# First key unit of an attention–MLP kernel loaded in two transfers, and fewer idle matmuls on TensorE at the start

## The chip, the cores and the metric

The kernel runs on one NeuronCore of a Trainium2 chip. The metric is device time in microseconds (us), from the start to the end of one launch. Five engines run side by side, each through its own list of instructions in order, and meet only through semaphores: TensorE (PE; its weight loads, PEld, overlap its matmuls), VectorE (DVE), ScalarE (ACT), GpSimd (POOL) and SyncE (SP), which issues nearly all transfers. The transfers run on 16 DMA engines.

## The reference

Attention with random features, then an MLP with softplus, all in float32:

```python
proj = np.einsum('bhsd,md->bhsm', x, omega)      # x = q*scale or k*scale
h = proj - np.sum(x * x, axis=-1, keepdims=True) / 2.0
h = h - np.max(h, axis=-1, keepdims=True)
phi = np.exp(h) / np.sqrt(m)
...
kv = np.einsum('bhsm,bhsd->bhmd', k_p, v)        # k_p = phi(k), q_p = phi(q)
z = np.sum(k_p, axis=2)
num = np.einsum('bhsm,bhmd->bhsd', q_p, kv)
den = np.einsum('bhsm,bhm->bhs', q_p, z)[..., None] + 1e-06
x = num / den                                    # attention, heads side by side
h = x @ w_in
out = (softplus(h)) @ w_out
```

There are 8 batches of 8 heads, 576 positions of 64 columns, 128 features; the MLP has 4608 tokens, 512 columns in and out and 2048 hidden columns. For one head of keys or queries a row needs its projection (a matmul), its norm (squares, then a sum) and the largest projection of the row before the exponential can run.

## The kernel before

Four heads form a *quad*; a batch has two quads (0 and 1 of batch 0 come first). The 576 positions of a quad are cut into five *units* of 128 positions (the last has 64). A unit of keys of batch 0 goes through this chain:

- SP loads it into one tile `xk` of 128 x 772 floats (`load`, L463): columns 0 to 255 are the keys transposed, for the projection; columns 256 to 511 are the keys in rows, for the norm; the rest are the values. One transfer, 386 KB.
- PE projects it (`project`, L491): four matmuls into two banks of PSUM, `ppk ... _0` and `_1`. The two banks come from a common store of eight.
- ACT (or POOL) squares the rows (L474, L476), DVE sums them (L481).
- DVE takes the maxima of the two banks (L541, twice), then two small steps (L548, L553) give the bias of the exponential.
- ACT runs the exponentials, two for each bank (L561). They write over the unit's tile, and a bank is free for a later unit when its two are done.
- PE multiplies the exponentials with the values (`outer`, L700 and L695, into `kt`, which takes one more bank).

Units come in the order quad 0 unit 0, quad 1 unit 0, quad 0 unit 1, quad 1 unit 1 and so on. In the names of the rows below, `xk_1_0` is quad 1, unit 0. After the ten units of keys come ten of queries (`xq`, `ppq`), mixed with the weights of the MLP (`rawi`, `rawo`, split into high and low parts on ACT at L373, L381 and L391 and on DVE at L375, L385, L391 and L394). Later batches and the MLP (L1049 to L1051 and L1109 to L1111) take the rest of the time; the loads of all of it follow on SP's one queue. The kernel keeps eight semaphores for transfers in turn, so SP issues a transfer only when the one eight places before it has landed.

The order on each engine is not written by hand: `in_order` plays the works against a table of costs and due times and gives one list, and each engine's part of it is fixed when the program is built. After that, `with_fill` puts idle matmuls (`fill`, L1582) ahead of a work of PE where the planner's own clock sees a gap: `n = int((t - last - FILL) / 0.2135)`, and for works before `DENSE` (12 us by that clock) which take a bank two more. They write into a bank that is free, or into the one that the work takes, and nobody reads them. Ten more stand in front of the first projection (`fill("at.0", 10, idle)`); those multiply a tile of zeros, the others the identity. `in_order` knows nothing of the fills.

Of the kernel before, what the change touches and what calls it, by code (L numbers as in the profile page):

```python
# [35 lines left out]
MARGIN = 0.0000  # L36
START = {"SP": 0.75, "ACT": 1.9, "PE": 4.6}
SLOW = 7.19
FILL = 0.3
DENSE = 12  # L40
PATIENCE = {"PE": 0.0000, "DVE": 0.00, "ACT": 0.1822, "POOL": 0.00, "SP": 3.0950}
LEAN = {"DVE": 0.2675, "POOL": 0.1608, "ACT": 0.00}
SPREAD = ((0, 10.51), (17, 12.01))
VW = 512 + 4 * (D + 1)
# [17 lines left out]
def by(key, due):  # L62

    return due + DUE[key][PHASE[0]]
# [192 lines left out]
def with_fill(out, held, banks, until, emit):  # L257

    last, all_ = None, []
    for i, w in enumerate(out):  # L260
        if w.engine == "PE":
            t = w.end - w.cost
            n = int((t - last - FILL) / 0.2135) if last is not None and t < until else 0
            if last is not None and t < DENSE and w.take:
                n += 2
            names = [
                b for b in banks if all(x1 <= last and g < i or x0 >= t and f >= i for x0, x1, f, g in held.get(b, []))
            ] if n > 0 else []
            names = names or [box[key] for _, box, key in w.take if box[key] in banks]
            if names and n > 0:  # L270
                all_.append((emit, names[0], n))
            last = w.end
        all_.append(w)
    return all_
# [3 lines left out]
def favor_softplus_kernel(ctx, tc, q0, k0, qx, kx, tx, vv, om, wi, wo, out):  # L278
    nc = tc.nc
# [10 lines left out]
    at = ctx.enter_context(tc.tile_pool(name="at", bufs=1))  # L290
# [4 lines left out]
    def bank(name, tag):  # L295
        return ps.tile([P, 512], F32, name=name, tag=tag, bufs=1)

    idle = at.tile([P, P], F32, name="idle", tag="x.0", bufs=1)
# [38 lines left out]
    def act(n, space=None):  # L337
        return (0.066 if space == PSUM else 0.105) + 0.000833 * n

    def dve(n, rate=1):  # L340
        return 0.068 + 0.001042 * n / rate
# [4 lines left out]
    def do(engine, cost, due, emit, **kw):  # L346

        on = dict(zip(engine, cost)) if isinstance(engine, tuple) else {engine: cost}
        w = Work(on, due, emit, **kw)
        works.append(w)  # L350
        return w
# [86 lines left out]
    def plan_unit(q, kind, us, due, early, other=None):  # L438

        u = us[0]  # L440
# [3 lines left out]
        if early:  # L444
            src = (k0 if kind == "k" else q0)[q.qd]
        else:
            src = (kx if kind == "k" else qx)[q.b - 1, q.qd]
        nt = 2 * len(us) if u < 4 else 2 if other else 1
        b2 = {}
        w, n = nt * P, 2 * nt  # L450
        b = {}

        def load():
            if early:

                x = const.tile([P, 2 * DM], F32, name=f"x{nm}", tag=b["x"], bufs=1)
                b["v"] = x[:, UW : UW + 4 * (D + 1)].rearrange("p (c d) -> p c d", d=D + 1)
                b["qt"] = x[:, UW : UW + 4 * P].rearrange("p (c t) -> p c t", t=P)
                b["xs"] = x[:, : 4 * D]
                b["ph"] = x[:, : n * M].rearrange("p (c m) -> p c m", m=M)  # L460
                b["raw"], b["nat"] = x[:, :w], x[:, w : 2 * w].rearrange("p (c d) -> p c d", d=D)
                if kind == "k":
                    nc.sync.dma_start(x[:, :VW], src[:, u * VW : (u + 1) * VW])  # L463
                else:
                    nc.sync.dma_start(x[:, : 2 * w], src[:, u * UW : u * UW + 2 * w])
                return
            x = at.tile([P, 2 * UW], F32, name=f"x{nm}", tag=b["x"], bufs=1)
            nc.sync.dma_start(x[:, : 2 * w], tx[other.n - NQ] if other else src[:, u * UW : u * UW + 2 * w])
            b["raw"], b["nat"] = x[:, :w], x[:, w : 2 * w].rearrange("p (c d) -> p c d", d=D)
# [52 lines left out]
        def first(e, t):  # L522
            if not t:
                for i, x in enumerate(to):
                    x["ph"] = at.tile([P, k, M], F32, name=f"ph{nm}_{i}", tag=x["phs"], bufs=1)
            (nc.scalar.copy if e == "ACT" else nc.vector.tensor_copy)(features(t), b["pr", t][:, :, 0])
# [28 lines left out]
        def exponent(j):  # L555
# [7 lines left out]
        size = P * 4 * (VW if early and kind == "k" else 2 * w)  # L563
        ld = do(
            "SP", dma(size), by("unit.load", due), load, behind=prev.get("load"),
            take=[("w" if early else "x", b, "x")], delay=DL, spare=2 if early else 0,
        )
# [27 lines left out]
        else:  # L595
# [12 lines left out]
            for t in range(nt):  # L608
# [4 lines left out]
                c = do(  # L613
                    ("ACT", "DVE"), (act(2 * M, PSUM), dve(2 * M)), by("unit.first", due), lambda e, t=t: first(e, t), after=[p], behind=e,
                    take=[] if t else phs,
                )
# [962 lines left out]
    def fill(tag, n, idle=ident):  # L1579
        t = bank("fill", tag)[:, :P]  # L1580
        for _ in range(n):
            nc.tensor.matmul(t, idle, idle, start=True, stop=True)  # L1582

    with tc.manual_schedule():
        fill("at.0", 10, idle)
        for w in with_fill(*in_order(works, room, AHEAD, MARGIN), room["any"], 70, fill):
            if isinstance(w, tuple):
                w[0](*w[1:])
                continue
            w.emit(w.engine) if len(w.on) > 1 else w.emit()  # L1590
# [99 lines left out]
```

## Time and profile before

| what | value |
|---|---|
| median of 3 runs (lowest, highest) | 1006.22 us (1006.0, 1007.1) |
| time of the profiled execution | 1006.46 us |
| its span, first to last instruction | 1004.7 us |
| busy: PE, DVE, ACT, POOL | 992.0, 805.4, 673.7, 79.8 us |
| moved | 113.81 MB, mean 113 GB/s over the span |

The span is what the rows below are taken from; 1.8 us of the execution's time lie outside it. Matmuls are pipelined and a row of PE counts idle matmuls as busy, so PE's 99% says little about how much of its time is needed. A matmul of float32 stands as two instructions in the trace (ten fills are x20). "Idle before" counts from the modelled end of the instruction ahead; on ACT and DVE instructions that follow each other overlap by some 0.1 us, start to start being shorter than their length.

### The profile page before, as it was taken

The page shows a single profiled execution, that of the slowest core. Times are in us where ns is not written, and L with a number is a line of the kernel's source. Part 1 is how long each engine was busy: PE and PEld are TensorE (multiplying, and loading weights), DVE is VectorE, ACT ScalarE, POOL GpSimd, SP SyncE. Part 2 cuts the span into 40 slices and gives each one's busy share as a digit, 9 for nine tenths or more (in the row PEclk, how much of TensorE's full clock was granted, in tenths as well). Part 3 has the DMA queues.
Part 4 walks back from the last instruction along what each step waited for, and adds up shares of the span by engine and source line. Part 5 has one row for each costly group of instructions (what it writes and reads, how often), then busy time and mean ns, then how long its engine had stood idle before and what let it go on. Part 6 is the DMA issues. An engine that isn't in the chain of part 4 may idle for free.

```text
span 1004.7 us, 17142 instructions
## 1 busy us (share of the span) xinstructions
PE 992.0 (99%) x5753; PEld 807.7 (80%) x5753; DVE 805.4 (80%) x2194; ACT 673.7 (67%) x1629; POOL 79.8 (8%) x90
## 2 busy tenths in 40 slices
PE   9999999999999999999999999999999999999998
PEld 8888888787778787887878787878788778788886
DVE  6999997988868787888888897979889846998600
ACT  6999987757677675666675756756576555777600
POOL 0113211000001000100000000100010000001000
PEclk9999999999999999999999999999999999999999
DMA  9963444443252424442343335243534121000011
GB/s 346 373 242 118 146 151 122 134 117 94 96 149 95 134 93 132 137 114 82 115 120 126 91 95 152 95 132 94 133 117 112 64 79 42 1 1 1 1 53 32
DMA packets 64334, 113.81 MB, mean 113 GB/s; under 512 B 18268, under 2 KB 37112, under 8 KB 64248
## 3 DMA queue, kind: packets, MB, share of 16 engines
q1 hardware_dynamic: 64088, 112.60, 36.1%
q8 instruction: 46, 0.75, 0.3%
q14 instruction: 40, 0.33, 0.1%
q10 hardware_dynamic: 160, 0.13, 0.1%
HBM read 85.68 MB, written 27.03 MB: 112 GB/s over the span
## 4 chain that ended last, share of the span: by engine, by line
PE 87%; DVE 6%; ACT 4%; DMA 1%; issue 1%; POOL 0%; DVEq 0%; ACTq 0%; SPq 0%
PE acc L1109 13%; PE acc L1110 12%; PE acc L1111 12%; PE h L1049 10%; PE h L1050 9%; PE h L1051 9%; PE ppk L491 3%; PE kt L655 3%; PE xp L977 3%; PE pb L1384 2%; PE ppq L516 2%; PE pc L1384 2%; PE pa L1384 1%; DMA xq<-qx 1%; PE fill L1582 1%
## 5 line engine op out<-in xcount | busy, mean ns | idle before, releaser
L1109 PE MATMUL acc<-wo,gh 128*128 128x512 f32 x512 | 204.1, 399 | 0.0
L1110 PE MATMUL acc<-wo,gh 128*128 128x512 f32 x512 | 200.2, 391 | 0.0
L1111 PE MATMUL acc<-wo,gl 128*128 128x512 f32 x512 | 199.7, 390 | 0.0
L1049 PE MATMUL h<-xh,wi 128*128 128x512 f32 (+1 forms) x512 | 190.8, 373 | 1.9 <-DVE u L1064 1.1
L1050 PE MATMUL h<-xl,wi 128*128 128x512 f32 (+1 forms) x512 | 186.1, 364 | 0.0
L1051 PE MATMUL h<-xh,wi 128*128 128x512 f32 (+1 forms) x512 | 185.8, 363 | 0.0
L1055 ACT ACTIVATE u<-h 128x512 f32<-128x512 f32 (+1 forms) x128 | 70.1, 547 | 81.4 <-PE h L1051 79.2
L1109 PEld LDWEIGHTS acc<-wo,gh 128*128 128x128 f32 x512 | 96.2, 188 | 24.9 <-issue 6.8
L1049 PEld LDWEIGHTS h<-xh,wi 128*128 128x128 f32 x512 | 96.4, 188 | 23.4 <-DVE u L1064 3.9
L1111 PEld LDWEIGHTS acc<-wo,gl 128*128 128x128 f32 x512 | 96.1, 188 | 21.2 <-DVE gl L1204 0.4
L1110 PEld LDWEIGHTS acc<-wo,gh 128*128 128x128 f32 x512 | 96.5, 188 | 15.9
L1051 PEld LDWEIGHTS h<-xh,wi 128*128 128x128 f32 x512 | 96.4, 188 | 15.4
L1050 PEld LDWEIGHTS h<-xl,wi 128*128 128x128 f32 x512 | 96.6, 189 | 13.5
L1064 DVE SCALAR_TENSOR_TENSOR u<-h,u 128x512 f32<-128x512 f32 (+1 forms) x128 | 79.2, 619 | 32.7 <-ACT u L1061 31.5
L1068 ACT CAST gh<-u 128x512 fp32r<-128x512 f32 (+1 forms) x101 | 57.2, 566 | 46.0 <-PE acc L1110 29.1
L1072 DVE TENSOR_TENSOR gl<-u,gh 128x512 fp32r<-128x512 f32 (+1 forms) x106 | 68.7, 648 | 14.9 <-ACT gh L1068 13.1
L1061 ACT ACTIVATE u<-u 128x512 f32<-128x512 f32 (+1 forms) x128 | 74.2, 580 | 3.9
L1058 ACT ACTIVATE u<-u 128x512 f32<-128x512 f32 (+1 forms) x128 | 74.3, 581 | 3.2
L887 DVE CUSTOM_DVE_ANT_0 junk<-phq,zb 128x128 bf16<-128x128 f32 (+1 forms) x228 | 67.4, 296 | 7.0 <-ACT phq L561 0.4
L538 ACT ACTIVATE phq<-phq,smq 128x128 f32<-128x128 f32 x194 | 59.5, 389 | 10.1 <-DVE smq L553 10.1
L561 ACT ACTIVATE phk<-ppk,smk 128x128 f32<-128x128 f32 x230 | 63.6, 375 | 3.3 <-DVE smk L553 3.1
L541 DVE TENSOR_REDUCE smk<-ppk 128x4 f32<-128x512 f32 (+2 forms) x80 | 46.0, 595 | 24.5 <-PE ppk L491 24.5
(217 smaller groups left out, 1764.2 us busy)
## 6 DMA issues: line engine op xcount, KB each, us to landing
xk<-kx SPq DMA_DIRECT2D x28, 512.0 KB, 3.8
xq<-qx SPq DMA_DIRECT2D x28, 512.0 KB, 3.6
fdq<-flq SPq DMA_DIRECT2D x28, 512.0 KB, 2.8
qq<-fdq SPq DMA_DIRECT2D x112, 128.0 KB, 2.9
rawi<-wi SPq DMA_DIRECT2D x16, 512.0 KB, 6.7
rawo<-wo SPq DMA_DIRECT2D x16, 512.0 KB, 10.1
out<-o SPq DMA_DIRECT2D x32, 256.0 KB, 2.1
v<-vv SPq DMA_DIRECT2D x14, 576.0 KB, 3.7
```

What stands on the lines that cost most here:

```text
L887: nc.vector.tensor_tensor_reduce(jk[r, c % jk.shape[1]], ph[r, c], q.zb[r, h], 1.0, 1e-6, ALU.mult, ALU.add, dn[r, 0, c : c + 1])
L1049: nc.tensor.matmul(b["h"], wh, xh[:, cc, t], start=cc == 0, stop=False)
L1050: nc.tensor.matmul(b["h"], wh, xl[:, cc, t], start=False, stop=False)
L1051: nc.tensor.matmul(b["h"], wl, xh[:, cc, t], start=False, stop=cc == NCC - 1)
L1055: nc.scalar.activation(b["u"], b["h"], AF.Abs)
L1058: nc.scalar.activation(b["u"], b["u"], AF.Exp, scale=-1.0)
L1061: nc.scalar.activation(b["u"], b["u"], AF.Ln, bias=1.0)
L1064: nc.vector.scalar_tensor_tensor(b["u"], b["h"], 0.0, b["u"], ALU.max, ALU.add)
L1072: (nc.vector if e == "DVE" else nc.gpsimd).tensor_tensor(b["gl"], b["u"], b["gh"].bitcast(F32), ALU.subtract)
L1109: nc.tensor.matmul(dst, gh, w2[fc][:, 0, c], start=start, stop=False, **kw)
L1110: nc.tensor.matmul(dst, gh, w2[fc][:, 1, c], start=False, stop=False, **kw)
L1111: nc.tensor.matmul(dst, gl, w2[fc][:, 0, c], start=False, stop=stop, **kw)
```

## The change

Three things change. The tile of quad 0 unit 0's keys is loaded by two transfers, columns 0 to 255 and then 256 to 771, in place of one. Six idle matmuls stand in front instead of ten. `FILL` goes from 0.3 to 1.0 and the `DENSE` rule is gone, so that the planner puts fewer idle matmuls ahead of later works.

```diff
-FILL = 0.3
-DENSE = 12
+FILL = 1.0
...
             n = int((t - last - FILL) / 0.2135) if last is not None and t < until else 0
-            if last is not None and t < DENSE and w.take:
-                n += 2
...
                 if kind == "k":
-                    nc.sync.dma_start(x[:, :VW], src[:, u * VW : (u + 1) * VW])
+                    for c in ((0, w), (w, VW)) if not q.qd and not u else ((0, VW),):
+                        nc.sync.dma_start(x[:, c[0] : c[1]], src[:, u * VW + c[0] : u * VW + c[1]])
...
-        fill("at.0", 10, idle)
+        fill("at.0", 6, idle)
```

The order of all other instructions is the same on PE, DVE, ACT, POOL and SP. Lines behind the edits move up by two or three (L491 is L489, L1582 is L1580). Three places show what moves.

PE at the start of the program, before:

```order
L1582 MATMUL fill<-idle 128x128 x10
L491 MATMUL ppk_0_0_0_115<-omf,xk_0_0_106 128x128
L491 MATMUL ppk_0_0_1_116<-omf,xk_0_0_106 128x128
L491 MATMUL ppk_0_0_0_115<-omf,xk_0_0_106 128x128
L491 MATMUL ppk_0_0_1_116<-omf,xk_0_0_106 128x128
L1582 MATMUL fill<-ident 128x128
L491 MATMUL ppk_1_0_0_130<-omf,xk_1_0_108 128x128
```

The same place after:

```order
L1580 MATMUL fill<-idle 128x128 x6
L489 MATMUL ppk_0_0_0_112<-omf,xk_0_0_102 128x128
L489 MATMUL ppk_0_0_1_113<-omf,xk_0_0_102 128x128
L489 MATMUL ppk_0_0_0_112<-omf,xk_0_0_102 128x128
L489 MATMUL ppk_0_0_1_113<-omf,xk_0_0_102 128x128
L489 MATMUL ppk_1_0_0_125<-omf,xk_1_0_105 128x128
```

Four idle matmuls are gone in front, and one between the first two projections; the two like it ahead of `xk_0_1` and `xk_1_1` are gone too. The first projection now waits for the first of the two transfers alone, by the program's semaphores.

PE from the end of the fourth projection (quad 1 unit 1) to the first product `kt`, before:

```order
L1582 MATMUL fill<-ident 128x128 x6
L491 MATMUL ppk_0_2_0_189<-omf,xk_0_2_123 128x128
L491 MATMUL ppk_0_2_1_190<-omf,xk_0_2_123 128x128
L491 MATMUL ppk_0_2_0_189<-omf,xk_0_2_123 128x128
L491 MATMUL ppk_0_2_1_190<-omf,xk_0_2_123 128x128
L1582 MATMUL fill<-ident 128x128 x5
L491 MATMUL ppk_1_2_0_216<-omf,xk_1_2_137 128x128
L491 MATMUL ppk_1_2_1_217<-omf,xk_1_2_137 128x128
L491 MATMUL ppk_1_2_0_216<-omf,xk_1_2_137 128x128
L491 MATMUL ppk_1_2_1_217<-omf,xk_1_2_137 128x128
L1582 MATMUL fill<-ident 128x128 x2
L700 MATMUL kt_0_237<-xk_0_0_106 128x65 x4
```

and after:

```order
L1580 MATMUL fill<-ident 128x128
L489 MATMUL ppk_0_2_0_175<-omf,xk_0_2_120 128x128
L489 MATMUL ppk_0_2_1_176<-omf,xk_0_2_120 128x128
L489 MATMUL ppk_0_2_0_175<-omf,xk_0_2_120 128x128
L489 MATMUL ppk_0_2_1_176<-omf,xk_0_2_120 128x128
L489 MATMUL ppk_1_2_0_196<-omf,xk_1_2_132 128x128
L489 MATMUL ppk_1_2_1_197<-omf,xk_1_2_132 128x128
L489 MATMUL ppk_1_2_0_196<-omf,xk_1_2_132 128x128
L489 MATMUL ppk_1_2_1_197<-omf,xk_1_2_132 128x128
L698 MATMUL kt_0_214<-xk_0_0_102 128x65 x4
```

Of thirteen idle matmuls one is left. Two further groups shrink later: eighteen become fifteen ahead of an MLP product near 61 us of the trace, and a single one near 72 us goes.

SP, its first transfers, before:

```order
L314 DMA omf_83<-om 128x128
L463 DMA xk_0_0_106<-k 128x772
L463 DMA xk_1_0_108<-k 128x772
L463 DMA xk_0_1_110<-k 128x772
L463 DMA xk_1_1_112<-k 128x772
```

and after:

```order
L311 DMA omf_83<-om 128x128
L461 DMA xk_0_0_102<-k 128x256
L461 DMA xk_0_0_102<-k 128x516
L461 DMA xk_1_0_105<-k 128x772
L461 DMA xk_0_1_107<-k 128x772
```

Every later transfer stands one place further back. ACT's square of the first unit waits for the second of the two.

## Rows read from the trace of the kernel before

**Rows 1.** Busy time by stage: stretch, its length, then busy (instructions) by engine, clock, DMA.

```profile
0.00:10.45 10.45, 9.17 (x58) 7.74 (x58) 4.96 (x22) 4.48 (x11) 0.70 (x6) 1.00 0.80 271
10.45:27.80 17.35, 17.18 (x154) 15.04 (x153) 14.30 (x56) 14.64 (x51) 0.80 (x2) 1.00 1.04 401
27.80:102.30 74.50, 71.54 (x597) 61.69 (x595) 72.85 (x213) 73.29 (x198) 16.70 (x15) 1.00 0.65 239
102.30:1004.70 902.40, 894.14 (x4949) 723.20 (x4948) 713.33 (x1906) 581.26 (x1371) 61.58 (x68) 1.00 0.32 96
```

**Rows 2.** Chain of waits over the first 30 us: start, length, what.

```profile
1.05 4.65 PE fill L1582 x20
...
5.75 1.20 PE ppk L491 x8
6.95 0.43 PE fill L1582 x2
...
7.42 0.72 PE ppk L491 x8
...
10.52 1.55 PE fill L1582 x12
...
12.90 1.32 PE fill L1582 x10
...
15.05 0.66 PE fill L1582 x4
...
15.75 1.11 PE kt L700 x8
...
27.82 0.39 ACT kvs L706
```

**Rows 3.** Waits of DVE and of ACT, 8 to 30 us: total, times, longest.

```profile
DVE smk L541 <- PE ppk L491: 3.2, 5, 1.1
...
ACT xk L561 <- DVE smk L553: 2.1, 3, 1.5
```

**Rows 4.** The fills' matmuls by operand: ns min/median/max, first and last start.

```profile
L1582 PE MATMUL fill<-ident x70: 271/275/377, 6.9 to 71.8; 128*128 128x128 f32 x70
...
L1582 PE MATMUL fill<-idle x20: 421/421/583, 1.1 to 5.3; 128*128 128x128 f32 x20
```

**Rows 5.** Timeline of ACT: start, length, what, idle before and what ended it.

```profile
4.54 0.42 ACT L474 ACTIVATE xk<-xk 128x256 f32<-128x256 f32 x1 [2.53 <-DMA xk<-k]
5.55 0.42 ACT L474 ACTIVATE xk<-xk 128x256 f32<-128x256 f32 x1 [0.59 <-DMA xk<-k]
...
8.47 0.42 ACT L474 ACTIVATE xk<-xk 128x256 f32<-128x256 f32 x1 [0.91 <-DMA xk<-k]
...
9.75 1.23 ACT L561 ACTIVATE xk<-ppk,smk 128x128 f32<-128x128 f32 x4
...
11.54 0.62 ACT L561 ACTIVATE xk<-ppk,smk 128x128 f32<-128x128 f32 x2 [0.26 <-DVE smk L553]
...
14.18 0.62 ACT L561 ACTIVATE xk<-ppk,smk 128x128 f32<-128x128 f32 x2 [0.37 <-DVE smk L553]
...
18.84 1.66 ACT L561 ACTIVATE xk<-ppk,smk 128x128 f32<-128x128 f32 x6 [1.48 <-DVE smk L553]
```

**Rows 6.** Timeline of DVE, the first two waits for a projection.

```profile
6.98 0.76 DVE L541 TENSOR_REDUCE smk<-ppk 128x2 f32<-128x256 f32 x2 [0.56 <-PE ppk L491]
...
12.86 0.42 DVE L541 TENSOR_REDUCE smk<-ppk 128x2 f32<-128x256 f32 x1 [1.08 <-PE ppk L491]
```

**Rows 7.** Timeline of SP's issues and of ACT, 22 to 28 us.

```profile
23.46 0.33 SPq L468 DMA_DIRECT2D xk<-kx  x1
...
25.46 0.41 ACT L474 ACTIVATE xq<-xq 128x256 f32<-128x256 f32 x1
26.38 1.14 ACT L561 ACTIVATE xq<-ppq,smq 128x128 f32<-128x128 f32 x4 [0.51 <-DVE smq L553]
```

**Rows 8.** Timeline of SP's first issues, and of DVE's first use of a transfer.

```profile
1.19 5.65 SPq L463 DMA_DIRECT2D xk<-k  x10
...
2.66 0.23 DVE L315 TENSOR_SCALAR omf<-omf 128x128 f32<-128x128 f32 x1 [1.42 <-DMA omf<-om]
```

## The prediction

> **What bounds the kernel now.** I read the busy time by stage first. The span has four stages [rows 1]. Up to 10.45 us the loads set the pace. From there to 27.8 us the chain of waits runs along PE without a break, but much of that chain is idle matmuls: ten in front (4.65 us), three single ones (0.43 us each), then groups of 1.55, 1.32 and 0.66 us between needed projections [rows 2]. From 27.8 to 102.3 us DVE is busy 72.85 and ACT 73.29 of 74.5 us: these two are the bound, and almost nothing there waits. From 102.3 us to the end PE is busy 894 of 902 us.
>
> So the question is what the change takes off before 27.8 us, and whether the two later stages pass it on. In the early stretch the waits say who holds whom: between 8 and 30 us DVE waits for nothing but projections, 3.2 us in five waits, and ACT waits 2.1 us for the biases that DVE makes of them [rows 3]. PE is what is late, and PE is late because it runs idle matmuls: that is the reader's first result. A fill marks PE busy in the trace while the data for the next projection has long landed.
>
> **The change part by part. In front.** Ten idle matmuls take 4.65 us, 0.465 each; four fewer end 1.86 us sooner, near 3.8 us. The first projection then needs the first 128 KB of its unit. From below: 64 KB issued at 0.74 us are used at 2.66 us, 1.9 us later [rows 8]; the new first transfer, issued near 1.2 us, can't land much before 3.1 us. From above: the whole unit is there at 4.54 us [rows 5]. I take 3.4 us, nearer to the small transfer. The projection runs from 3.9 to 5.1 us (1.20 us as before [rows 2]) in place of 5.75 to 6.95 us.
>
> What is that worth? Little. DVE takes the maxima of the first projection only behind the sum of the second unit's squares, and that unit lands at 5.55 us; square and sum end near 6.4 us. DVE's wait of 0.56 us before 6.98 us [rows 6] goes, no more. Without the split the projection would run from 4.6 to 5.8 us, still before 6.4 us. And ACT's square at 8.47 us has waited 0.91 us for its transfer [rows 5]: up to there landings are the bound, and nothing done on PE moves them. I cost the split and the four fills at nothing; the landings hide them, and 0.56 us is the most that they are worth.
>
> The split's price: one more issue on SP. Ten issues of keys take 5.65 us [rows 8], so each later key is issued 0.5 us later, onto a queue that is ahead of its transfers: units land 1.0 us apart or more from 4.54 us on [rows 5], and the sixth is issued before the second has landed. Between 0 and 0.5 us on every later landing; I take 0.1 us, because the queue is full, and allow nothing below zero, since the bytes are the same.
>
> **From 8.47 us to 18.84 us.** Here ACT is the engine to follow. It has three waits, 0.26, 0.37 and 1.48 us, 2.11 us in all [rows 5]. Six exponentials take 1.66 us at 18.84 us, so they start 0.25 us apart and are 0.39 us long; a wait counted from the end of the one ahead hides that overlap of 0.14 us, three times. Without waits ACT stands at 18.84 - 2.11 - 0.42 = 16.3 us, 2.5 us sooner. Do the three biases come in time?
>
> - The first (11.54 us) needs DVE 0.4 us sooner. DVE has won the 0.56 us above. Yes.
> - The second (14.18 us) hangs on the fifth projection. It stood behind six fills, from 10.52 to 12.07 us [rows 2]. Its two banks are free when the first two of the four exponentials at 9.75 us are done, near 10.4 us [rows 5]. So its last three matmuls now run from 10.4 to about 11.05 us, and DVE's maxima start at 11.2 us in place of 12.86 us [rows 6]; the bias is 1.6 us sooner and ACT wants it 0.9 us sooner. Yes.
> - The third (18.84 us, after 1.48 us) hangs on the seventh. Ahead of it now: sixth projection, whose second bank ACT gives back at 12.16 - 0.37 = 11.8 us, done at 12.45 us; the first product `kt`, whose bank comes 0.8 us later, 12.65 to 13.75 us (15.75 to 16.86 us before [rows 2]); then the seventh, done at 14.6 us in place of 17.5 us. DVE's steps between it and the bias took 1.25 us, so 15.85 us; ACT is free at 16.3 us. In time, with 0.45 us to spare.
>
> So ACT gains 2.5 us, PE 2.9 us, and PE no longer holds anyone. DVE could gain 2.9 us, but its work on the first weights (L385) follows ACT's (L381): 2.5 us for it too.
>
> **What is late next: landings.** The loads keep the DMA queues full (share 1.04 [rows 1]) and don't move. SP's issue at 23.46 us waited for the transfer eight places ahead, the queries that ACT squares at 25.46 us [rows 7]: 2.0 us of slack, so ACT's gain falls to 2.0 us there. But ACT then waited 0.51 us for a bias at 26.38 us. Its start is now 23.45 + 0.3 by the landing, 26.38 - 2.5 = 23.9 by the bias: the 2.5 us are back.
>
> **The sum.** 2.5 us, less 0.1 us for later landings: 2.4 us. Upper end: ACT's waits up to 26.38 us altogether, 2.5 + 0.5 = 3.0 us. Lower end, with 0.5 us for the landings: 2.0 us. From 27.8 to 102.3 us DVE and ACT are full and in fixed order, so they pass a shift on, and transfers that wait for buffers follow; the fewer fills near 61 and 72 us cost and give nothing, since the bound there is DVE (at most four of them, 1 us, if it were PE). From 102.3 us PE passes it on. The profiled execution takes 1006.46 us; 2.4 us less is 1004.06 us. The median lies 0.24 us below the profiled one, 1006.22 us: I forecast **1003.8 us**.
>
> **The rivals. TensorE's clock stays low for longer.** The row says: the fills in front last 421 ns, later ones 275 ns [rows 4]; the first projection 1.20 us, the second 0.72 us [rows 2]. [...] Now PE pauses at 5.1, 6.8 and 7.9 us and later. Up to 10.4 us a low clock is free: projections of 1.2 us fit between landings. [...]
>
> [...]
>
> [...]
>
> **The split delays all keys.** If two transfers cost the queue the full 0.5 us, ACT's row at 8.47 us moves by that and 2.0 us are left: 1004.2 us. Against it: landings 1.0 us apart for 386 KB leave no room for a fixed cost for each transfer.
>
> [...]
>
> **The gain is given back between 28 and 102 us.** A landing or a buffer that I took to follow does not; DVE then shows new waits, 0.3 to 2 us of them: 1004.1 to 1005.8 us. Against it: the slack of 2.0 us was the shortest I found.
>
> **How the numbers follow.** Forecast (1003.2 to 1004.4 us): 0.60. Clock low for longer, gain partly or wholly lost: 0.16. Split delays the keys: 0.07. Given back later: 0.10. Slower: 0.07. A difference of 0.2%, 2.0 us, is about what a measurement of this kernel can tell from none; faster by more means under 1004.2 us. That takes in most of the first case (0.54) and a little of the split's and of the third (0.04): 0.58 faster, 0.36 same, 0.06 slower. The range of 8 in 10 runs from 1003.2 us to 1005.8 us.
>
> **What would show it.** After the change: first projection near 3.9 us; DVE's five waits for projections nearly gone; ACT's exponentials of 18.84 us at 16.4 us; first `kt` near 12.7 us; the stage that began at 27.8 us begins near 25.4 us, and DVE and ACT stay full up to 100 us. Fills or projections at double length behind 11 us would show the clock; a square at 8.47 us that moves later, the split. I am wrong if ACT reaches its place of 18.84 us in time and the end does not follow.

## The result, and the profile after

The changed kernel takes 1017.85 us (median of five runs, 1012.17 to 1018.41) against 1006.48 us for the kernel before on the same chip (five runs, 1006.0 to 1008.05). The ratio is 1.0099, 95% interval 1.0071 to 1.0127: slower, where 1003.8 us was forecast and the range ended at 1005.8 us. The profiled execution takes 1017.58 us with a span of 1015.8 us. Four of the five runs show a mean granted clock of 0.979 or 0.980; the shortest, 1012.17 us, shows 1.0. Ratios here and below leave out runs more than 1.5% above the fastest of the same kernel, which concerns six runs of e12 and one of e4.

The first table to read is the busy time by stretch (columns: stretch in us, its length, busy us and instructions of PE, PEld, DVE, ACT and POOL, granted clock, DMA share, GB/s). The stretches are cut at 4.30 us, where the lengths of PE's matmuls change, where the granted clock changes and where the last stage begins.

```profile
0.00:4.30 4.30, 3.19 (x14) 2.90 (x16) 1.05 (x8) 1.28 (x1) 0.70 (x6) 1.00 0.49 137
4.30:7.72 3.42, 1.28 (x16) 0.89 (x16) 1.49 (x4) 0.83 (x2) 0.00 (x0) 1.00 1.01 333
7.72:48.68 40.96, 40.62 (x212) 35.96 (x213) 26.73 (x99) 25.94 (x81) 0.80 (x2) 0.50 0.92 355
48.68:115.24 66.56, 62.64 (x521) 53.71 (x520) 63.40 (x181) 64.81 (x176) 16.75 (x15) 1.00 0.50 170
115.24:1015.80 900.56, 893.00 (x4949) 723.13 (x4948) 712.54 (x1906) 582.26 (x1371) 61.65 (x68) 1.00 0.33 96
```

From 7.72 to 48.68 us the granted clock is 0.50, called the low level below, and 1.00 the full one. In the first stretch the column stands at 1.00, but its twelve fill matmuls last 434 ns on average; two in the stretch at 0.50 last 492 ns, and thirty behind 48.68 us, at 1.00, 278 ns. So a low level at the start of a program is inferred from lengths, here and in [rows 4], and the column does not show it. Between 7.72 and 48.68 us PE is busy 40.62 of 40.96 us while DVE and ACT fall to 26.73 and 25.94 us. In the kernel before they were the bound from 27.8 us on, with PE behind them [rows 1]; now PE is the bound up to 48 us. The last stage is as it was, some 900 us.

The chain of waits of the changed kernel shows the same from inside (start, us, what):

```profile
8.01 2.19 PE ppk L489 x16
10.19 0.74 PE fill L1580 x2
10.97 2.61 PE ppk L489 x16
13.59 1.90 PE kt L698 x8
15.48 1.16 PE ppk L489 x8
...
37.72 1.16 PE ppq L489 x8
38.88 1.90 PE nuq L814 x8
40.77 1.71 PE tpq L801 x8
...
49.21 0.38 ACT kvs L704
```

The first product takes 1.90 us in the chain (1.11 before), a projection 1.16 us (0.72 before) [rows 2], and the chain stays on PE from 8 to 48 us. What PE did ahead of the fall stands in its timeline (start, length, work, and in brackets the idle time ahead of it and what ended that):

```profile
3.13 0.85 PE L1580 MATMUL fill<-idle 128*128 128x128 f32 x3
4.04 0.82 PE L489 MATMUL ppk<-omf,xk 64*128 64x128 f32 x8
6.22 0.71 PE L489 MATMUL ppk<-omf,xk 64*128 64x128 f32 x8 [1.35 <-DMA xk<-k]
8.01 2.19 PE L489 MATMUL ppk<-omf,xk 64*128 64x128 f32 x16 [1.07 <-DMA xk<-k]
```

The first projection (0.82 us) starts at 4.04 us with two matmuls of 484 ns on average, low by their length, the second takes 0.71 us, and then come two pauses for data, 1.35 and 1.07 us. The granted clock falls from 1.00 to 0.50 in the second of them, at 7.72 us, and the third and fourth projection take 2.19 us together. Behind the first, one takes 0.72 us in the kernel before [rows 2].

Until the low clock tells, ACT shows the gain that was forecast beginning:

```profile
7.99 0.42 ACT L472 ACTIVATE xk<-xk 128x256 f32<-128x256 f32 x1 [1.37 <-DMA xk<-k]
8.94 0.42 ACT L472 ACTIVATE xk<-xk 128x256 f32<-128x256 f32 x1 [0.54 <-DMA xk<-k]
...
17.98 1.40 ACT L559 ACTIVATE xk<-ppk,smk 128x128 f32<-128x128 f32 x5 [0.93 <-DVE smk L551]
```

Two of the three waits of [rows 5] are gone, the third is 0.93 in place of 1.48 us, and the exponentials of 18.84 us begin at 17.98 us: 0.86 us sooner. A marker later on is one `h` matmul with 256 columns that PE runs just ahead of the last stage, after a wait of 0.33 us for `u`. Before and after:

```profile
102.77 0.39 PE L1049 MATMUL h<-xh,wi 128*128 128x256 f32 x1 [0.33 <-DVE u L1064]
```

```profile
115.68 0.38 PE L1047 MATMUL h<-xh,wi 128*128 128x256 f32 x1 [0.33 <-DVE u L1062]
```

It is 12.91 us late. So the whole loss, and more, arises between the exponentials near 18 us and the marker; from the marker to the end the kernel before takes 1004.7 - 102.77 = 901.9 us and the changed one 900.1 us.

### The profile page after: what moved, and what is told of

Same layout as the page of the kernel before. It is cut to its first block, busy times and chain, and to the rows that moved or that the text cites. A ratio compares the mean times of both kernels' runs of the same rounds, so it can differ in the third digit from the quotient of the medians.

```text
span 1015.8 us, 17046 instructions
## 1 busy us (share of the span) xinstructions
PE 1000.7 (99%) x5707; PEld 816.6 (80%) x5707; DVE 805.2 (79%) x2194; ACT 675.1 (66%) x1629; POOL 79.9 (8%) x90
## 4 chain that ended last, share of the span: by engine, by line
PE 88%; DVE 5%; ACT 4%; DMA 1%; issue 1%; SPq 0%; DVEq 0%; ACTq 0%
PE acc L1107 12%; PE acc L1108 12%; PE acc L1109 12%; PE h L1047 10%; PE h L1048 9%; PE h L1049 9%; PE ppk L489 3%; PE xp L975 3%; PE kt L653 3%; PE pb L1382 2%; PE ppq L514 2%; PE pc L1382 1%; PE kt L698 1%; PE pa L1382 1%; PE ppq L489 1%
## 5 line engine op out<-in xcount | busy, mean ns | idle before, releaser
L1048 PEld LDWEIGHTS h<-xl,wi 128*128 128x128 f32 x512 | 96.6, 189 | 13.6
```

The source lines that it names most:

```text
L1048: nc.tensor.matmul(b["h"], wh, xl[:, cc, t], start=False, stop=False)
```

## Experiments

All kernels are the kernel before or the changed one with a part put back or another count of idle matmuls. Three theories stood at the start. **A**: the idle matmuls between the early projections hold the clock, and the needed work, once the clock has fallen, does not raise it. **B**: six in front are too few. **C**: the split makes the first projection so early that PE pauses behind it.

| run | what it is | us (median, lowest to highest, runs) | ratio to before, 95% interval |
|---|---|---|---|
| e1 | before, split alone | 1006.84 (1005.8 to 1007.5, 10) | 1.0001, 0.9991 to 1.0010 |
| e2 | before, six in front alone | 1007.98 (1007.12 to 1008.66, 10) | 1.0014, 1.0004 to 1.0023 |
| e3 | before, the planner's numbers alone | 1011.12 (1002.22 to 1016.45, 10) | 1.0049, 1.0024 to 1.0075 |
| e4 | changed, one transfer | 1014.82 (1002.41 to 1017.57, 10) | 1.0064, 1.0034 to 1.0094 |
| e5 | before, early counts 1 1 1 3 3 2 | 1002.70 (1002.18 to 1005.22, 7) | 0.9971, 0.9960 to 0.9982 |
| e6 | before, early counts 1 1 1 1 0 0 | 1002.16 (1001.26 to 1012.62, 12) | 0.9968, 0.9950 to 0.9985 |
| e7 | before, early counts 0 0 0 6 5 2 | 1003.83 (1003.03 to 1004.61, 10) | 0.9976, 0.9967 to 0.9985 |
| e8 | before, early counts 0 0 0 1 0 16 | 1008.92 (1006.99 to 1011.33, 8) | 1.0025, 1.0014 to 1.0036 |
| e9 | e5 with the split | 1003.83 (1002.96 to 1005.34, 11) | 0.9978, 0.9969 to 0.9987 |
| e10 | changed, early counts as before | 1005.90 (1003.92 to 1009.78, 11) | 0.9998, 0.9987 to 1.0010 |
| e11 | before, early counts 0 0 0 3 3 2 | 1003.80 (1002.82 to 1004.54, 9) | 0.9976, 0.9967 to 0.9986 |
| e12 | e5 with the split and six in front | 1013.64 (1004.16 to 1024.91, 12) | 0.9997, 0.9986 to 1.0007 |

The early counts are the idle matmuls ahead of the second, third, fourth, fifth and sixth projection and of the first `kt`; before they are 1 1 1 6 5 2 [rows 2]. The kernel before ran beside them: 1006.29 us (median of 31) for e1 to e4, 1006.26 us (28) for e5 to e8, 1006.07 us (32) for e9 to e12. The ratios need not be the quotients of the medians.

**One part at a time: e1, e2, e3, e4.** The edits:

```diff
e1:
-                    nc.sync.dma_start(x[:, :VW], src[:, u * VW : (u + 1) * VW])
+                    for c in ((0, w), (w, VW)) if not q.qd and not u else ((0, VW),):
+                        nc.sync.dma_start(x[:, c[0] : c[1]], src[:, u * VW + c[0] : u * VW + c[1]])
e2:
-        fill("at.0", 10, idle)
+        fill("at.0", 6, idle)
e3:
-FILL = 0.3
-DENSE = 12
+FILL = 1.0
+DENSE = 0
e4, against the changed kernel:
-                    for c in ((0, w), (w, VW)) if not q.qd and not u else ((0, VW),):
-                        nc.sync.dma_start(x[:, c[0] : c[1]], src[:, u * VW + c[0] : u * VW + c[1]])
+                    nc.sync.dma_start(x[:, :VW], src[:, u * VW : (u + 1) * VW])
```

> The kernel before with the split of the first unit's load alone; all idle matmuls stay. Theory A (the idle matmuls between the first projections hold TensorE's clock up; without them it falls near 7.7 us and stays low to 48.7 us): clock as before, double lengths up to some 6.9 us only, time 1006.0 to 1006.8 us; the landings behind the first unit 0.5 us later than before (second unit 6.1 us in place of 5.5 us). Theory B (ending the unbroken run in front after six fills is what costs the clock): the same time. Theory C (the split delays the second unit, and the longer pause drops the clock): about 1017 us.

> The kernel before with six idle matmuls in front in place of ten, nothing else. Theory A: the singles and groups behind the projections still hold the clock, time 1005.5 to 1007 us. Theory B: about 1017 us, with matmuls of double length from near 8 us to near 48 us. Theory C: 1005.5 to 1007 us.

> The kernel before with the planner's new rule alone (a single idle matmul ahead of the fifth projection in place of sixteen in the first 16 us); ten in front, one transfer. Theory A: about 1017 us, double lengths to near 48 us. Theory B: the clock rises with the ten in front and stays, and the 2.5 us of the prediction come: about 1004 us. Theory C: about 1004 us.

> The changed kernel with the first unit loaded in one transfer. Theory A and theory B: about 1017 us, as the changed kernel. Theory C: about 1004 us, with the clock up from 7 us on. By all three ACT's square of the second unit is back at 5.55 us (6.2 us in the changed kernel).

The split alone and six in front alone cost 0.0 and 0.14%. The planner's numbers alone cost 0.5%, and the changed kernel without its split still loses 0.6% and falls to a granted clock of 0.50 at 11.45 us: C falls as the cause, A stands. Of the whole loss, 1.0%, the planner's numbers alone give about half; what the two other parts add beside them was not taken apart further. The clock is read in the busy time by stretch, of e3 and of e4, again cut where it changes:

```profile
0.00:12.53 12.53, 9.96 (x73) 8.55 (x73) 7.37 (x34) 7.02 (x20) 0.70 (x6) 1.00 0.84 309
12.53:46.66 34.13, 34.13 (x176) 30.28 (x175) 21.29 (x76) 20.55 (x65) 0.80 (x2) 0.50 0.93 358
46.66:102.00 55.34, 52.37 (x451) 45.30 (x450) 52.80 (x153) 54.29 (x148) 12.42 (x10) 1.00 0.54 189
```

```profile
11.45:49.00 37.55, 37.48 (x190) 33.10 (x188) 23.65 (x84) 23.36 (x73) 0.80 (x2) 0.50 0.91 350
```

In e3 PE is busy for the whole 34.13 us at the low level, without one pause, and the clock stays down. Each of these kernels also did the opposite once: one run of ten took 1002.22 us (e3) and 1002.41 us (e4), with a mean granted clock of 0.999. So the same program either loses the clock (1010 to 1018 us) or keeps it, and then it is 4 us faster than before: the gain that was forecast is there, under the loss. Among e4's long runs 1017.57 and 1017.41 us show a mean clock of 0.981, 1011.44, 1011.77 and 1013.67 us 0.986 or 0.987: the low stretch comes in more than one length. Four others (1011.85 to 1017.10 us) show 0.999 or 1.0, as the changed kernel's run of 1012.17 us does, so for these the clock as the cause is argued from their lengths, not shown.

In e2 the clock rises late, by the lengths: behind its six fills PE waits 0.93 us for the unit, and up to 8.9 us two projections take 1.23 us and two single fills 0.79 us each, in place of 0.72 and, in the same view, 0.49 us. From 4.00 to 15.16 us 51 instructions keep PE busy for 10.02 us, 196 ns for each; behind it 42 take 4.72 us, 112 ns for each. That costs 1.7 us at the end of its span (1006.4 against 1004.7 us). B has a small part. The wait alone does not decide it: e4 has the same six fills and a wait of 0.92 us, and its first projection takes 0.71 us.

**How many idle matmuls hold the clock: e5, e6, e7.** The first counts that the planner finds are overwritten, shown for e5:

```diff
+EARLY = [1, 1, 1, 3, 3, 2]
...
             if names and n > 0:
+                n = EARLY.pop(0) if EARLY else n
                 all_.append((emit, names[0], n))
```

> The kernel before with the early idle matmuls ahead of projections 2 to 6 and of the first product set to 1, 1, 1, 3, 3, 2 in place of 1, 1, 1, 6, 5, 2; ten in front, one transfer. Theory A (PE's pauses between the projections drop the clock, the needed work behind them does not raise it again, and the prediction's gain is there wherever the clock stays up): the three or five pieces taken away are 1.2 us of the chain; if the singles and the shorter groups hold the clock, 1005 us, all runs together; if not, runs spread from 1002 to 1017 us as with the rule changed alone. Rival D (any group shorter than before loses the clock): a spread with a median over 1009 us.

> The kernel before with 1, 1, 1, 1, 0, 0 early idle matmuls: the singles between the first four projections stay, the groups behind them go as in the change. If the pauses up to 10 us are what drops the clock: up throughout, 1002.5 to 1004 us. If the pauses between 9 and 12 us (the fifth and sixth projection waiting for banks) drop it: a spread, 1002 to 1017 us, double lengths from near 12 us.

> The kernel before with 0, 0, 0, 6, 5, 2 early idle matmuls: no singles, all groups. If the pauses up to 10 us drop the clock: the groups behind them (near 9.2 to 15.7 us) raise it again or come too late; a spread of 1006 to 1012 us. If only the later pauses matter: 1006.3 us like the kernel before, since the groups still stand in PE's way.

All three beat the kernel before, and the granted clock of their profiles is 1.00 in every stretch; by the lengths it is up in e5 at 5.29 us (first projection 0.71 us), in e6 at 7.54 us (second, 0.71 us) and in e7 at 8.59 us at the latest (fourth, 0.72 us). Rival D falls: e5 shows a mean clock of 1.0 in seven of seven runs. e5 and e7 came out 2.3 and 2.5 us below what theory A and the second case had for them (1005 and 1006.3 us). Halving the groups (e5) is worth 0.29%; with the singles and next to no groups (e6) it is 0.32%, but one of twelve runs took 1012.62 us with a mean clock of 0.986. In e5 DVE's waits for projections between 8 and 30 us are down from 3.2 us in five [rows 3], and ACT's exponentials of 18.84 us start 2.06 us sooner. Its row of DVE's waits (us, times, longest), and its marker:

```profile
DVE smk L543 <- PE ppk L493: 1.3, 3, 0.6
```

```profile
100.81 0.38 PE L1051 MATMUL h<-xh,wi 128*128 128x256 f32 x1 [0.33 <-DVE u L1066]
```

The marker is 1.96 us sooner: what ACT gained at 16.78 us (2.06) reaches the last stage almost whole.

**What raises a fallen clock: e8.** Here `EARLY = [0, 0, 0, 1, 0, 16]`, a long run of idle matmuls ahead of the first product. **A1** says that these raise a fallen clock where needed work does not; **A2** that a fallen clock stays down for some 35 us whatever PE does.

> The changed rule (a single early idle matmul; ten in front, one transfer) with sixteen idle matmuls ahead of the first product, where the clock had just fallen (12.5 us). Theory A1 (at the low level the products and projections of this stretch, 64 rows or 65 columns, do not raise the clock, full idle matmuls do): up again by 20 us in place of 46.7 us; sixteen at the low level cost 7.4 us, so 1007 to 1011 us and no run over 1013 us. Rival A2 (a fallen clock stays low for some 35 us whatever runs): low to near 47 us and sixteen more matmuls in the way, 1018 to 1022 us for most runs.

The busy time by stretch of e8, cut at the clock's changes and at the first idle matmul of the group, and its idle matmuls between 11.19 and 19.03 us (count, busy us, mean ns):

```profile
8.00:11.19 3.19, 2.53 (x20) 1.93 (x20) 3.19 (x14) 3.12 (x11) 0.00 (x0) 1.00 1.04 411
11.19:12.53 1.34, 1.15 (x6) 0.93 (x6) 1.20 (x8) 1.34 (x7) 0.00 (x0) 0.50 1.02 410
12.53:18.02 5.49, 5.49 (x26) 5.49 (x26) 1.81 (x7) 3.53 (x14) 0.40 (x1) 0.50 1.04 399
18.02:19.03 1.01, 0.95 (x10) 0.76 (x8) 0.00 (x0) 0.00 (x0) 0.00 (x0) 1.00 1.06 396
19.03:30.00 10.97, 10.97 (x100) 9.77 (x102) 8.69 (x33) 7.44 (x25) 0.40 (x1) 1.00 1.04 401
```

```profile
L1584 PE MATMUL fill<-ident 128*128 128x128 f32 x32 | 6.4, 393 | 0.0
```

The clock falls at 11.19 us as in e4 (11.45), and comes back at 18.02 us, inside the idle group, after 5.49 us of it; then it stands at 1.00 to the end. A2 falls. Needed work kept PE just as busy in e3, 34.13 of 34.13 us at 0.50, without that effect. The eight runs took 1006.99 to 1011.33 us, as A1 had it; A2 had 1018 to 1022 us. A1 stands: in e8 and e3 these two kinds of work differ for a fallen clock although both read as a busy PE. What in them makes the difference was not tried.

The same needed work also ran at 1.00. In the kernel before no idle matmul runs between the last of the early groups and 61 us, and ahead of that the products and projections alone fill PE (its busy time in one stretch):

```profile
15.75:27.80 12.05, 12.05 (x110) 10.72 (x111) 10.71 (x42) 9.98 (x35) 0.40 (x1) 1.00 1.05 398
```

PE is as full there as in e3 behind 12.53 us, with the same work, and the granted clock is 1.00 in place of 0.50. The two kernels differ only in their idle matmuls. In these two profiles the work stays at the level at which it starts, 12.05 us at 1.00 and 34.13 us at 0.50.

**The split and the front with the clock held: e9, e10, e11, e12.** e9 is e5 with e1's edit, e12 is e9 with e2's, e10 is the changed kernel with the planner's numbers of before, e11 is e5 with `EARLY = [0, 0, 0, 3, 3, 2]`.

> The kernel before with shortened groups of idle matmuls (one, one, one, three, three and two ahead of the early projections, ten in front), plus the change's split of the first unit. It prices the split where PE is out of the way and the idle matmuls keep the clock. The prediction's step (0.1 us, at most 0.5, on every later landing of the keys): 1002.8, at most 1003.2 us, against 1002.7 us without the split. The rival that two transfers cost the queue more than that: 1003.3 us or later, and ACT's third square (8.47 us in the trace of before) about 0.5 us later than in the run without the split. If the split were worth what the first projection gains by it: 1002.2 us or less.

> The changed kernel with the idle matmuls ahead of the early projections put back as they were before; the split and the six in front stay. If the gaps alone cost the clock (theory A), the clock rises once, at some point up to 16 us, and holds: 1006 to 1008.5 us, like the runs with the split alone and with six in front alone. If a shorter run in front, together with the first projection sooner, costs the clock too (theory B come back), some runs take over 1010 us with a clock below 0.99.

> The kernel before with ten idle matmuls in front, none ahead of the second to fourth projections, and three, three and two ahead of the fifth, the sixth and the first product. PE pauses for data between 7 and 9 us and is nearly unbroken behind it. If pauses before 9 us are harmless as long as idle matmuls follow (as in the run without the singles, 1003.83 us), the clock holds and the time is that of the shortened groups: 1002 to 1003 us. If the clock falls after such pauses and only long groups kept it, runs at 1008 to 1017 us appear.

> The changed kernel with one, one, one, three, three and two idle matmuls put ahead of the early projections: eleven in place of none and of twenty. If the gaps alone decide, the prediction's gain is there: 1002 to 1004 us, 1002.7 us as with ten in front and one transfer. If six in front raise the clock late (15 us in the run with six alone), about 1004 to 1006 us; if the shorter front makes the clock fall, over 1010 us.

e9 against e5 prices the split where PE holds nobody up. ACT's square of the fourth unit and its exponentials, in e5 and then in e9:

```profile
8.25 0.42 ACT L476 ACTIVATE xk<-xk 128x256 f32<-128x256 f32 x1 [1.04 <-DMA xk<-k]
...
16.78 1.66 ACT L563 ACTIVATE xk<-ppk,smk 128x128 f32<-128x128 f32 x6 [0.58 <-DVE smk L555]
```

```profile
9.09 0.42 ACT L477 ACTIVATE xk<-xk 128x256 f32<-128x256 f32 x1 [0.58 <-DMA xk<-k]
...
17.48 1.66 ACT L564 ACTIVATE xk<-ppk,smk 128x128 f32<-128x128 f32 x6 [0.33 <-DVE smk L556]
```

The landing is 0.84 us later and the exponentials 0.70 us; the medians, 1003.83 and 1002.70 us, differ by 1.1 us, the ratios by 0.0007, within their intervals. Landings also scatter from run to run (that square stands between 7.86 us in e11 and 8.92 us in e4 without the split, and between 8.33 us in e12 and 9.15 us in e1 with it), so 0.7 us is one pair's price. Over all fourteen profiles that square stands at 8.32 us on average without the split (nine) and at 8.83 us with it (five): an estimate of 0.5 us. That the price is above 0.1 us is likely, and no comparison here shows a gain.

e10 has six in front, the split and the long groups: no run over 1010 us and a ratio of 0.9998, so with the idle matmuls back the loss is gone: A holds in the changed kernel itself. Three of its eleven runs (1005.90, 1008.05 and 1009.78 us) show a mean clock of 0.996 or 0.997, near the 0.996 of e8's profile with its low stretch of 6.83 us; what the clock did in them is not shown. e11 leaves the three singles out: 1003.80 us where 1002 to 1003 us was expected, a mean clock of 0.999 or 1.0 in all nine runs, though PE pauses for data before 9 us here too (0.29 us ahead of the fourth projection) and again behind the fourth (0.43 us). Its ACT rows (the fourth unit's square and the exponentials) and its marker are the forecast's own places:

```profile
7.86 0.42 ACT L476 ACTIVATE xk<-xk 128x256 f32<-128x256 f32 x1 [0.59 <-DMA xk<-k]
...
16.27 1.66 ACT L563 ACTIVATE xk<-ppk,smk 128x128 f32<-128x128 f32 x6 [0.34 <-DVE smk L555]
```

```profile
100.19 0.38 PE L1051 MATMUL h<-xh,wi 128*128 128x256 f32 x1 [0.33 <-DVE u L1066]
```

e12 differs from e9 only by four idle matmuls in front, and it falls apart in two: six of its runs took 1004.16 to 1007.48 us, six 1019.80 to 1024.91 us. e9 had nothing of the kind in eleven runs. Three of the long runs show a mean clock of 0.982 or 0.983, as a lost clock would; three show 0.999 or 1.0, and all six are longer than any run with a lost clock above (1018.41 us). The profiled execution of e12 was a short one, so what happened in the long ones stays open, and nothing is built on them. The short ones alone put e12 0.2% behind e9 (ratios 0.9997 and 0.9978, intervals just touching), as six in front cost e2 0.14%. Whether B is also a partner of A, fewer in front making a fall more likely where few follow, is not shown.

## Why the prediction was wrong, step by step

**The step that failed is the rival on the clock**, which had 0.16 and, as the slower case, 0.07. It took a low clock as free up to 10.4 us and so asked when the clock would rise. The question was whether it holds. By the lengths it rose near 4.30 us, sooner than in the kernel before [rows 2], and the granted clock fell to 0.50 at 7.72 us. Needed work filled PE from 8 us on, products from 13.6 us on: PE was busy 40.62 of 40.96 us, the clock stayed down, and the rise came at 48.68 us. The kernel before could show needed work at a granted clock of 1.00 (15.75 to 27.80 us), but no row of it has needed work behind a fall, so none could show whether it raises the clock again; the bound for that had to be taken much wider.

**What the low level cost.** e4's run of 1017.41 us lies 15.0 us above its run with the clock held, for a low stretch of 37.55 us in its profile, 0.40 us for each us (that run and the profiled one have a mean clock of 0.981). e3's profiled run lies 13.05 us above its run with the clock held, for 34.13 us: 0.38. The groups do not double at 0.50: `kt` takes 1.90 us in place of 1.11, 0.79 us more, which is 0.42 us for each us at the low level, and that fits; a projection takes 1.16 us in place of 0.72, a fill's two matmuls 0.74 us in place of 0.43 [rows 2].

**In front.** The first projection starts at 4.04 us (forecast 3.9). That it gains nothing is right as far as the runs go: e10, with the split, six in front and the other idle matmuls back, stands at 0.9998. (e1, at 1.0001, has ten in front and tests the split alone.) That the four fills in front cost nothing was wrong: 0.14% alone (e2), where by the lengths the clock rose late and the landings did not hide it.

**The split's price** of 0.1 us was probably too small: 0.7 us in the pair e5 and e9, 0.5 us by the averages of all profiles, which is the upper end that was given. In the kernel before, the medians don't show it (e1). The argument of landings 1.0 us apart, with no room for a cost of each transfer, was not borne out. It would have moved the forecast by about half a us.

**ACT's three waits, 2.5 us.** Right in kind, somewhat large. Where the clock held, e11's exponentials start at 16.27 us (forecast 16.3), 2.57 us sooner, and DVE's waits for projections are down to 0.9 us in two. But that the number agrees to a tenth is in part luck: the fourth unit's square stands at 7.86 us there, 0.61 us sooner than before (8.47 us [rows 5]), and a wait of 0.34 us is left. In e5 (2.06 us sooner) one of 0.58 us is left; in e6, with the groups gone as in the change, the first of the three, which the forecast had as gone:

```profile
11.65 0.63 ACT L563 ACTIVATE xk<-ppk,smk 128x128 f32<-128x128 f32 x2 [0.26 <-DVE smk L555]
```

So about 2 us are won here (2.06 us in e5; e6's marker stands at 100.87 us, 1.90 us sooner), some 0.5 us less than the sum had.

**Passing it on.** Right up to 102 us: e11's marker is 102.77 - 100.19 = 2.58 us sooner, and e5's 1.96 us of 2.06, so the rival "given back" falls. e11's first landings were sooner too, so it is no test of the slack of 2.0 us. From the marker to the end it takes 901.0 - 100.19 = 900.8 us against 901.9 us before: 1.1 us more are won there, in e5 1.8 us, where the forecast had nothing. One place of that can be seen, waits of PE in the kernel before around 283 us, which neither e5 nor e11 needs and e1 keeps (columns as in DVE's waits):

```profile
PE ppq L516 <- DVE spq L509: 0.4, 2, 0.3
PE ppq L516 <- ACT phk L561: 0.2, 1, 0.2
```

Why a shift removes them was not tried.

So the gain that was computed is there to about half a us where the clock holds, and the last stage adds to it; e3 and e4 then take 1002.2 and 1002.4 us. The time was wrong by 14 us because a quantity that the whole sum assumed, the clock, did not hold without the idle matmuls that the change took out.

## What to carry to other kernels

Idle matmuls on a path are not waste until it is shown that the clock holds without them: first cut groups by half and keep one ahead of each early work (e5: 0.29% faster than before, seven runs of seven), and only then go further, over ten runs or more, since a kernel at the edge loses the clock in one run of twelve (e6) and was not always short with six in front (e12). When a step is priced by the clock, price both a late rise (1.7 us in e2) and a fall (15.0 us in e4). A full PE does not tell which level it has: here the same work filled it for 12.05 us at 1.00 in one kernel and for 34.13 us at 0.50 in another (e3). The split of a transfer paid nothing here and put the later landings back by about 0.5 us (an estimate); ask first who waits for the first part.

## What was not expected of the hardware

- PE busy 34.13 of 34.13 us (e3) and 40.62 of 40.96 us (changed kernel) at granted clock 0.50, and no rise; in e8 it rose behind 5.49 us of idle matmuls. The kernel before is busy 12.05 of 12.05 us with the same work at 1.00.
- The rise at the end of the low stretch came at 46.66, 48.68 and 49.00 us in three kernels whose falls lay at 12.53, 7.72 and 11.45 us. By then transposes (`tpq`, `xfq`) and `nuq` had taken the place of most of the first products and projections in the chain; whether these raised it is not shown.
- The same program keeps or loses the clock from run to run: 1002.41 us with a mean clock of 0.999 and 1017.57 us with 0.981 in e4.
- With the same ten in front, the first projection takes 0.71 us in the chain of e5 and 1.23 us in that of e6 (1.20 us before [rows 2]): by these lengths the first rise of the clock comes ahead of it in one execution and behind it in another.
